# Batch 1's keys and values loaded behind the first units, their maxima taken by TensorE, and an undivided fp32 value product in a fused attention and feed-forward kernel

## The chip, the cores and the metric

The kernel runs on one core of a Trainium2 chip. The metric is device time in microseconds (us) of one execution; less is better. Three runs of the kernel before gave 734.79, 735.6 and 737.56 us, median 735.6 us.

## What is computed

Attention with a learned position bias, followed by a layer norm and a feed-forward block with a residual. There are 4 batches, 8 heads, 576 positions and a head size of 64; d_model is 512 and the feed-forward width 2048. Everything is float32. Cut to what matters:

```python
scores = scale * np.matmul(q, k.transpose(0, 1, 3, 2))
x = (psi_rel / psi_i)[..., None]            # logs of distances and positions
bias = np.maximum(x @ w1 + b1, 0.0) @ w2    # (576, 576, 8)
scores = scores + bias.transpose(2, 0, 1)[None]
attn = softmax(scores);  attn_out = np.matmul(attn, v)
x = attn_out.transpose(0, 2, 1, 3).reshape(B, S, H * D)
xn = (x - mu) / np.sqrt(var + 1e-06) * g_ln
out = x + np.maximum(xn @ w_ch1, 0.0) @ w_ch2
```

## The kernel before, in words

**Units.** Attention is done in 144 units. A unit is one batch, one chunk `c` of 128 query positions and one head; chunk 4 holds only 64 positions, so there a unit takes two heads. The list `ORD` sets their order: units 0 to 3 are batch 0's chunk 4, units 4 to 7 batch 1's chunk 4, units 8 to 15 batch 0's chunk 0, units 16 to 23 batch 1's chunk 0, and so on; batches 2 and 3 come from unit 72 on. One unit is: scores on PE (`qk`, L406, into `sps`), bias added and row minimum taken on DVE (L426, tile `t`), exponential on ACT (L430), transposition of the weights of attention, and the value product on PE into `xps` (`pv`).

**Bias.** The bias is worked out once, for all batches, in 36 groups of 16 rows: relu on ACT and DVE (`bias_relu`), fp32 matmuls on PE (`bias_mm`, L220 and L197, into `bps`), evacuation on ACT (`ev`), a DMA write to a DRAM buffer (`nb<-ev`). A unit reads its 128 x 576 piece back (`ldb<-nb`). Six groups are done ahead of the first unit, the others between the units.

**Value products of two kinds.** Where `nat_pv` holds (batch 0's chunks 4 and 0, batch 1's chunk 4, that is units 0 to 15) the values are used as they came, in fp32 (`vf`), with weights of attention transposed by PE; elsewhere the values are split into a high and a low fp16 part and PE does three times as many fp16 products (`pv_mms`, L497). In the fp32 kind `pv` takes the 128 query columns in two halves `e` of 64: five matmuls of 64 stationary columns for each half, so ten for a unit (L527).

**Splitting the values.** `split_v(b, g)` handles two heads' values. DVE reduces their absolute maximum along each partition (L365, `vam`); the maximum over partitions is taken for batches 0 and 1 by GpSimd (L369, a partition all-reduce into `var`), for batches 2 and 3 by PE and DVE in `part_max`: a PE transposition (L135), a DVE reduce (L138), a DVE product with a corner of the identity (`pdg`, L139), a PE matmul with a row of ones (L141), a DVE copy (L381). Its PSUM bank there is `y1` of `ps_y`, which the transposed weights of attention use too. Then follow some one-column operations on DVE (`pow2`, `c8`), the high part on ACT (L385) and the low part on DVE (L374). `w_scale` uses `part_max` too, once for each of four groups of feed-forward weights.

**Loads.** A sorted list `loads` says at which unit a tile is due, and `issue_loads(u)` issues what is due by `u + 6`. Keys (`kf`), values (`vf`, later `ldv`) and queries (`qf`) go through GpSimd's (POOL's) queue; bias pieces (`ldb`), bias writes (`nb`) and feed-forward weights (`wend`) through SP's. The keys of batches 0 and 1 are held back until a given one of the first six bias groups is evacuated (`gate`); the values are not. The pools of keys and values hold nine tiles each, so those of batches 0 and 1 fit at once.

**Feed-forward.** For each block of 128 positions, `ffn_w1` does 48 fp16 matmuls at a time into the only bank of `ps_h` (`hps`, L719), ACT (L724) and DVE (L727) read it out, and `ffn_w2` does 12 matmuls into `y` (L747). These are put between the units, so many a unit. The weights come packed and are unpacked (L653, L655, L657) and split (L692, L695) by DVE and ACT during the first 32 units.

The instructions of one engine run in the order in which they stand in its list. That order is not the order of the source: a scheduler lays the program out, so that a change in one place can move instructions in others.

Of the kernel before, what the change touches and what calls it, by code (L numbers as in the profile page):

```python
# [8 lines left out]
F32 = mybir.dt.float32  # L9
# [6 lines left out]
ALU = mybir.AluOpType  # L16
# [6 lines left out]
def kernel(  # L23
# [58 lines left out]
    id_sb = const.tile([128, 128], F32)  # L82
    one_sb = const.tile([2, 128], F32)
    gs_sb = const.tile([128, 512], F32)
# [49 lines left out]
    def part_max(am, n, ps):  # L134
        T.transpose(ps[0:n, 0:128], am, id_sb)  # L135
        mx = small.tile([2, 1], F32, tag="pmx", name="pmx")
        dg = small.tile([2, 2], F32, tag="pdg", name="pdg")
        V.tensor_reduce(out=mx[0:n], in_=ps[0:n, 0:128], op=ALU.max, axis=AX.X)  # L138
        V.tensor_scalar(out=dg[0:n, 0:n], in0=id_sb[0:n, 0:n], scalar1=mx[0:n], scalar2=None,  # L139
                        op0=ALU.mult)  # L140
        T.matmul(out=ps[:, 128:128 + n], lhsT=one_sb[0:n], rhs=dg[0:n, 0:n], start=True, stop=True)  # L141
        return ps[:, 128:128 + n]

    rt = {}
    evi, ttri = {}, {}
# [127 lines left out]
    for b in range(NB):  # L273
        if b < 2:
            tf = ustart[b, 4] == ub[b]
            for g in range(4):
                loads.append((ub[b] + (g if tf else 2 * g) - (3 if b == 0 else 4), "k", (b, g)))
                if npt[b]:
                    loads.append((ub[b] + ((-3, -1, 0, 1) if tf else (-3, 1, 3, 5))[g], "w", (b, g)))
        else:  # L280
            for g in range(4):
                loads.append((ub[b] + 2 * g - 8, "k", (b, g)))
        if not npt[b] or not KEEPV[b]:
            for g in range(4):
                loads.append((uv[b] - 13 + 3 * g, "v", (b, g)))
        for c in range(4):
            for hh in range(2):
                loads.append((ustart[b, c] + 4 * hh - 3, "q", (b, c, hh)))
        loads.append((ustart[b, 4] - 3, "q", (b, 4, 0)))
# [5 lines left out]
    def issue_loads(u):  # L295
# [4 lines left out]
        while loads and out_ld[0] < LD and loads[0][0] <= u + 6:  # L300
            need, kind, key = loads[0]
            if kind == "k":
# [3 lines left out]
                if gate_on[0]:  # L306
                    gate.append((ld, 1 * key[1] + 0 + 2 * key[0]))
                kt[key] = raw
                continue
            if kind == "q":  # L310
# [11 lines left out]
            if kind == "w":  # L322
# [4 lines left out]
                if gate_on[0]:  # L327
                    gate.append((ld, 0 * key[1] + -9 + 0 * key[0]))
                vraw[key] = raw
                continue  # L330
            if kind == "b":
# [25 lines left out]
    def split_v(b, g):  # L357
# [8 lines left out]
        if kept and 0:  # L366
            after(red, evi[gorder[min(NP, 0 + 6) - 1]])
        if kept:
            G.partition_all_reduce(ar, am, channels=128, reduce_op=bass_rust.ReduceOp.absmax)  # L369
# [9 lines left out]
        def hi():  # L379
            if not kept:  # L380
                V.tensor_copy(ar, part_max(am, 1, ps_y.tile([128, 512], F32, tag="y1", name="pmv")))  # L381
            pow2(ar, vs, None)
# [130 lines left out]
    def pv(u):  # L513
# [7 lines left out]
        if c < 4:  # L521
            if nat_pv(b, c):
                vf = vraw[b, h // 2].rearrange("p (a b c) -> p a b c", a=2, b=5)[:, h % 2]
                for e in range(2):
                    for j in range(5):
                        n = 128 if j < 4 else 64
                        T.matmul(out=o[64 * e:64 * e + 64, h, :],  # L527
                                 lhsT=p[0:n, 128 * j + 64 * e:128 * j + 64 * e + 64],
                                 rhs=vf[0:n, j], start=(j == 0), stop=(j == 4))
            else:  # L530
                pv_mms([(o[:, h, :], p, vt[b, h // 2][:, h % 2])])
# [291 lines left out]
    if True:  # L823
# [16 lines left out]
        V.memset(mhalf, -0.5)  # L840
        V.memset(one_sb, 1.0)
        V.memset(half2, 0.5)
# [173 lines left out]
```

## Time and profile before

| | us |
|---|---|
| runs (3) | 734.79, 735.6, 737.56; median 735.6 |
| profiled execution, its own time | 739.38 |
| its span in the profile | 737.6 |
| PE busy (matmuls) | 679.2 (92%) |
| DVE busy | 492.5 (67%) |
| ACT busy | 381.3 (52%) |
| POOL busy | 64.5 (9%) |

PE is TensorE's matmul side, PEld its weight loads, DVE VectorE, ACT ScalarE, POOL GpSimd, SP SyncE. A busy time is the time in which the engine had at least one instruction under way. The ends of matmuls are modelled, so the time from one start to the next tells more than the length of one. The span is the time from the first to the last instruction; the execution's own time is 1.8 us longer.

### The profile page before, as it was taken

The numbers are of one execution on the slowest core, as the hardware profiler recorded it, in microseconds if no ns is written. First come the engines' busy times: TensorE is split into PE (matmuls) and PEld (weight loads), VectorE is DVE, ScalarE is ACT, GpSimd is POOL, SyncE is SP. The second block draws the span as 40 slices with busy tenths as digits, with TensorE's granted clock in tenths as the row PEclk, the third lists the DMA queues.
The fourth block names the chain that finished last, engine by engine and source line by source line (L and its number), as shares of the span: only waits on it lengthen the run. The fifth ranks groups of instructions, "written<-read, shape, count | busy, mean of one in ns | idle before, by whom it ended". The sixth has DMA issues, their size and how long they took to land.

```text
span 737.6 us, 20228 instructions
## 1 busy us (share of the span) xinstructions
PE 679.2 (92%) x8308; PEld 471.7 (64%) x8308; DVE 492.5 (67%) x1168; ACT 381.3 (52%) x789; POOL 64.5 (9%) x120
## 2 busy tenths in 40 slices
PE   4299899798699999999999999999999999999994
PEld 3156666464455677777777777776777777776772
DVE  5657788887848576758777575777766765755221
ACT  4367796776659744445455444445444554441110
POOL 3400101100000000111100010100000000001000
PEclk9689999899999999999999999999999999999998
DMA  8987779799945697777876665857666866532100
GB/s 264 318 266 243 242 229 233 196 279 247 211 100 134 161 194 176 179 163 183 192 181 161 152 153 154 172 122 183 160 153 160 175 159 145 131 55 47 30 16 14
DMA packets 153680, 124.13 MB, mean 168 GB/s; under 512 B 118900, under 2 KB 119156, under 8 KB 153588
## 3 DMA queue, kind: packets, MB, share of 16 engines
q1 hardware_dynamic: 147154, 103.00, 57.7%
q0 software_dynamic: 5440, 19.40, 8.4%
q8 instruction: 65, 1.06, 0.6%
q10 hardware_dynamic: 994, 0.44, 0.2%
q14 instruction: 27, 0.22, 0.1%
HBM read 79.38 MB, written 15.63 MB: 129 GB/s over the span
## 4 chain that ended last, share of the span: by engine, by line
PE 78%; DMA 10%; DVE 5%; issue 3%; ACT 2%; POOL 1%; SPq 0%; ACTq 0%; POOLq 0%; DVEq 0%
PE hps L719 24%; PE y L747 23%; PE sps L406 10%; PE xps L497 7%; PE ptm L468 3%; PE bps L220 3%; DMA ldb<-nb 2%; DMA pt<-e 2%; PE bps L197 2%; DMA wend<-in_w_ch_dram 2%; DMA ldv<-in_v_p_dram 1%; PE xps L545 1%; DMA nb<-ev 1%; PE xps L527 1%; DMA b_sb<-in_b_r_dram 1%
## 5 line engine op out<-in xcount | busy, mean ns | idle before, releaser
L719 PE MATMUL hps<-xT,w 128*128 128x128 f16 x3240 | 201.0, 221 | 3.8 <-DVE w L695 2.4
L719 PEld LDWEIGHTS <-w 128*128 128x128 f16 x3240 | 186.7, 99 | 15.5 <-issue 7.0
L747 PE MATMUL y<-w,hh 128*128 128x512 f16 x810 | 188.1, 379 | 1.5 <-DVE x L758 1.1
L430 ACT ACTIVATE t<-t,m 128x576 f32<-128x576 f32 x144 | 111.0, 771 | 120.4 <-DVE m L426 120.3
L747 PEld LDWEIGHTS <-hh 128*128 128x128 f16 x864 | 79.6, 98 | 86.6 <-issue 2.2
L426 DVE CUSTOM_DVE_ANT_0 t<-sps,ldb 128x576 f32<-128x576 f32 x144 | 105.5, 752 | 14.7 <-PE sps L406 7.3
L406 PE MATMUL sps<-kf,qf 64*128 64x288 f32 (+1 forms) x640 | 100.8, 441 | 7.3 <-DMA kf<-in_k_s_dram 6.7
L497 PEld LDWEIGHTS <-pt 128*128 128x128 f16 (+1 forms) x1904 | 64.3, 100 | 40.9 <-issue 27.6
L724 ACT ACTIVATE hh<-hps 128x512 f16<-128x512 f32 x72 | 42.7, 593 | 84.1 <-PE hps L719 84.0
L497 PE MATMUL xps<-v,pt 128*128 128x64 f16 (+1 forms) x1904 | 77.0, 194 | 8.3 <-DMA pt<-e 8.3
L758 DVE SCALAR_TENSOR_TENSOR x<-y,ycs,x 128x512 f32<-128x512 f32 x72 | 53.8, 747 | 43.9 <-PE y L747 43.3
L727 DVE SCALAR_TENSOR_TENSOR hh<-hps,hh 128x512 f16<-128x512 f32 x72 | 49.4, 687 | 46.4 <-ACT hh L724 46.3
L406 PEld LDWEIGHTS sps<-kf,qf 64*128 64x128 f32 (+1 forms) x640 | 48.8, 178 | 35.8 <-issue 17.1
L473 ACT ACTIVATE pt<-ptm 128x512 f16<-128x512 f32 x56 | 33.2, 592 | 73.1 <-PE ptm L468 73.0
L482 DVE SCALAR_TENSOR_TENSOR e<-t,e 128x512 f16<-128x512 f32 x72 | 49.7, 690 | 22.2 <-ACT e L439 22.1
L179 ACT ACTIVATE r<-psi_sb,pr_sb 128x496 f32<-128x496 f32 (+31 forms) x91 | 53.0, 640 | 7.8 <-DVE pr_sb L123 4.0
L439 ACT ACTIVATE e<-t 128x576 f16<-128x576 f32 x72 | 48.7, 676 | 0.8
L316 POOL DMA_DIRECT2D qf<-in_q_main_dram x32 | 18.5, 579 | 335.7 <-PE sps L406 284.0
L476 DVE SCALAR_TENSOR_TENSOR pt<-ptm,pt 128x512 f16<-128x512 f32 x56 | 38.5, 687 | 8.6 <-ACT pt L473 8.5
L220 PE MATMUL bps<-r,nw_sb 128*32 128x296 f32 (+31 forms) x450 | 35.1, 374 | 4.1 <-DVE r L181 3.6
L468 PE MATMUL ptm<-id_sb,t 128*128 128x128 f32 x224 | 34.2, 275 | 0.8 <-ACT t L430 0.8
L468 PEld LDWEIGHTS ptm<-id_sb,t 128*128 128x128 f32 x224 | 25.9, 141 | 9.0 <-issue 2.1
(118 smaller groups left out, 664.8 us busy)
## 6 DMA issues: line engine op xcount, KB each, us to landing
ldb<-nb SPq DMA_DIRECT2D x128, 288.0 KB, 3.5
wend<-in_w_ch_dram SPq DMA_DIRECT2D x29, 512.0 KB, 4.9
nb<-ev SPq DMA_DIRECT2D x34, 296.0 KB, 3.9
qf<-in_q_main_dram POOLq DMA_DIRECT2D x32, 256.0 KB, 4.0
kf<-in_k_s_dram POOLq DMA_DIRECT2D x16, 288.0 KB, 5.5
ldb<-nb SPq DMA_DIRECT2D x32, 144.0 KB, 4.6
out_dram<-x SPq DMA_DIRECT2D x17, 256.0 KB, 2.1
vf<-in_v_p_dram POOLq DMA_DIRECT2D x8, 320.0 KB, 6.4
```

What stands on the lines that cost most here:

```text
L179: S.activation(r[:, 0:n], psi_sb[:, 0:n], AF.Relu, bias=pr_sb[:, g4:g4 + 1], scale=1.0)
L220: T.matmul(out=ps[32 * s:32 * s + 32, hf, a - lo:b - lo], lhsT=nw2_sb, rhs=src, start=True, stop=True)
L406: T.matmul(out=o, lhsT=l, rhs=kk, start=True, stop=True, tile_position=(64 * hf, 64 * e))
L426: ttri[u] = V.tensor_tensor_reduce(out=halves(t), in0=ps[:, :, 0:HS], in1=halves(bias), scale=-0.125, scalar=3e38, op0=ALU.add, op1=ALU.mi ...
L430: S.activation(t, t, AF.Exp, bias=m, scale=-1.0, accum_out=l8[b, c][:, h:h + 1])
L468: T.transpose(pm[:, 128 * j:128 * j + 128], t[:, 128 * j:128 * j + 128], id_sb)
L482: V.scalar_tensor_tensor(out=e16[:, 640:1152], in0=t[:, 0:512], scalar=E_SCALE, in1=e16[:, 0:512], op0=ALU.mult, op1=ALU.subtract)
L497: T.matmul(out=o, lhsT=p[:, m], rhs=v[:, j, a, :], start=(i == 0), stop=(i == len(ops) - 1))
L719: T.matmul(out=h[:, idx * n:idx * n + n], lhsT=w[:, wo + kk * 128:wo + kk * 128 + 128], rhs=xT[k][:, xo + kk, 0:n], start=(i == 0), stop=( ...
L727: V.scalar_tensor_tensor(out=hh[:, 1], in0=h, scalar=0.0, in1=hh[:, 0], op0=ALU.max, op1=ALU.subtract)
L747: T.matmul(out=yps[k][t], lhsT=hh[:, a, o:o + 128], rhs=w[:, wo:wo + 512], start=(f == f0 and i == 0), stop=(f == f1 - 1 and i == 2))
L758: V.scalar_tensor_tensor(out=x, in0=y, scalar=ycs[:, g:g + 1], in1=x, op0=ALU.mult, op1=ALU.add)
```

## The change

1. `loads`: keys of batch 1 are due at units 6, 6, 7, 7 in place of 0 to 3, its values at 7, 7, 8, 8 in place of 1, 3, 4, 5. They are issued while the first units run, and each waits for the newest L426 (`ttri`) of the program at that place.
2. `split_v`: GpSimd's all-reduce is kept for batch 0 only. Batch 1 goes through `part_max`, as batches 2 and 3 do, and all three use the bank of `ps_h` in place of `y1`.
3. `part_max`: the DVE product `pdg` and the row of ones are gone; PE takes the maximum itself, repeated 128 times, as stationary operand, and the corner of the identity as moving one.
4. `pv`, chunks 0 to 3: the fp32 value product is done with all 128 columns at once, five matmuls for a unit in place of ten. Of the units of this kind that holds for eight, 8 to 15. Chunk 4's are as they were.

```diff
     def part_max(am, n, ps):
         T.transpose(ps[0:n, 0:128], am, id_sb)
         mx = small.tile([2, 1], F32, tag="pmx", name="pmx")
-        dg = small.tile([2, 2], F32, tag="pdg", name="pdg")
         V.tensor_reduce(out=mx[0:n], in_=ps[0:n, 0:128], op=ALU.max, axis=AX.X)
-        V.tensor_scalar(out=dg[0:n, 0:n], in0=id_sb[0:n, 0:n], scalar1=mx[0:n], scalar2=None,
-                        op0=ALU.mult)
-        T.matmul(out=ps[:, 128:128 + n], lhsT=one_sb[0:n], rhs=dg[0:n, 0:n], start=True, stop=True)
+        T.matmul(out=ps[:, 128:128 + n], lhsT=mx[0:n].to_broadcast([n, 128]), rhs=id_sb[0:n, 0:n],
+                 start=True, stop=True)
         return ps[:, 128:128 + n]
...
             for g in range(4):
-                loads.append((ub[b] + (g if tf else 2 * g) - (3 if b == 0 else 4), "k", (b, g)))
+                loads.append((ub[b] + g - 3 if b == 0 else 6 + g // 2, "k", (b, g)))
                 if npt[b]:
-                    loads.append((ub[b] + ((-3, -1, 0, 1) if tf else (-3, 1, 3, 5))[g], "w", (b, g)))
+                    loads.append((ub[b] + (-3, -1, 0, 1)[g] if b == 0 else 7 + g // 2, "w", (b, g)))
...
+                if key[0] == 1:
+                    after(ld, ttri[max(ttri)])
...
-        if kept:
+        if b == 0:
             G.partition_all_reduce(ar, am, channels=128, reduce_op=bass_rust.ReduceOp.absmax)
...
-            if not kept:
-                V.tensor_copy(ar, part_max(am, 1, ps_y.tile([128, 512], F32, tag="y1", name="pmv")))
+            if b > 0:
+                V.tensor_copy(ar, part_max(am, 1, ps_h.tile([128, 512], F32, tag="h", name="pmv")))
...
-                for e in range(2):
-                    for j in range(5):
-                        n = 128 if j < 4 else 64
-                        T.matmul(out=o[64 * e:64 * e + 64, h, :],
-                                 lhsT=p[0:n, 128 * j + 64 * e:128 * j + 64 * e + 64],
-                                 rhs=vf[0:n, j], start=(j == 0), stop=(j == 4))
+                for j in range(5):
+                    n = 128 if j < 4 else 64
+                    T.matmul(out=o[:, h, :], lhsT=p[0:n, 128 * j:128 * j + 128],
+                             rhs=vf[0:n, j], start=(j == 0), stop=(j == 4))
```

What the scheduler makes of it shows in the engines' lists. A row there is a line of the kernel, an operation, its output and inputs, and the output's size; xN is N of them in a row. The line numbers of the changed kernel are some lower.

POOL's list, from the first load of a key on. Before: the keys of batch 0 and of batch 1 (and one tile of batch 2, in the ninth place of the pool), with the all-reduces among them.

```order
L305 DMA kf<-in_k_s_dram 128x576
L369 ISA
L369 ISA var<-vam 128x1 x2
L305 DMA kf<-in_k_s_dram 128x576
L369 ISA var<-vam 128x1
L305 DMA kf<-in_k_s_dram 128x576 x7
L369 ISA var<-vam 128x1 x5
```

The change, from the same place on: the four keys of batch 0 and two of batch 1, two values of batch 1, two more keys of batch 1 and that of batch 2, a query, the other two values.

```order
L302 DMA kf<-in_k_s_dram 128x576 x6
L324 DMA vf<-in_v_p_dram 128x640 x2
L302 DMA kf<-in_k_s_dram 128x576 x3
L315 DMA qf<-in_q_main_dram 128x512
L324 DMA vf<-in_v_p_dram 128x640 x2
```

No all-reduce stands between the keys any more, and batch 1's four values are no longer among the first loads but behind its keys.

DVE's list. Before, in the opening, ahead of the first unit: the maxima of the values among the relus of the bias.

```order
L365 TENSOR_REDUCE vam<-vf 128x1
L181 TENSOR_SCALAR rp<-psi_sb,npr_sb 128x560
L181 TENSOR_SCALAR r<-psi_sb,npr_sb 128x576 x2
L181 TENSOR_SCALAR r<-psi_sb,npr_sb 128x560 x2
L365 TENSOR_REDUCE vam<-vf 128x1
L112 TENSOR_SCALAR var<-var 128x1
L365 TENSOR_REDUCE vam<-vf 128x1
L112 TENSOR_SCALAR var<-var 128x1
L365 TENSOR_REDUCE vam<-vf 128x1
L181 TENSOR_SCALAR rp<-psi_sb,npr_sb 128x528
L112 TENSOR_SCALAR var<-var 128x1
L113 TENSOR_SCALAR vs<-var 128x1
```

The change, between unit 20's L426 and unit 21's (a piece of it): the maxima of the values stand among the unpacking and splitting of weights.

```order
L136 TENSOR_REDUCE pmx<-pmv 1x1
L366 TENSOR_REDUCE vam<-vf 128x1
L534 TENSOR_TENSOR x<-xps,rl 128x512
L654 SCALAR_TENSOR_TENSOR w_148<-wend,w_148 128x512
L694 SCALAR_TENSOR_TENSOR w_141<-w_142,ws,w_141 128x512
L483 SCALAR_TENSOR_TENSOR e_1647<-t,e_1647 128x512
L485 SCALAR_TENSOR_TENSOR e_1647<-t,e_1647 128x64
L178 TENSOR_SCALAR r<-psi_sb,npr_sb 128x304
L656 SCALAR_TENSOR_TENSOR w_147<-wend,w_147 128x512
L382 COPY var<-pmv 128x1
```

All eight reduces left the opening, batch 0's too, which the diff does not touch: four stand behind units 3 to 6 now, four behind units 15 to 20. Of the eight low parts of values (L374), one stood in the opening, five behind units 7 to 13 and two behind units 15 and 17; now all eight stand behind units 17 to 26.

PE's list, at the first of batch 2's maxima. Before: the transposition into `pmv` stands in the middle of 48 matmuls of `hps` (each with its weight load).

```order
L719 LDWEIGHTS w_145
L719 MATMUL hps<-xT,w_145 128x128
L135 MATMUL pmv<-id_sb,vam 1x128
L719 LDWEIGHTS w_145
L719 MATMUL hps<-xT,w_145 128x128
```

The change: it stands behind a block of `y`, with a unit's transposition and scores between.

```order
L746 MATMUL y_4905<-w_139,hh 128x512
L469 MATMUL ptm<-id_sb,t 128x128 x4
L407 MATMUL sps<-kf,qf 128x288 x4
L498 LDWEIGHTS pt
L498 MATMUL xps<-v,pt 128x64
L134 MATMUL pmv<-id_sb,vam 1x128
```

The matmul that ends this maximum in the change, 87 rows on, among the next unit's transpositions and scores:

```order
L498 LDWEIGHTS pt
L498 MATMUL xps<-v,pt 128x64
L469 MATMUL ptm<-id_sb,t 128x128
L137 MATMUL pmv<-id_sb,pmx 128x1
L469 MATMUL ptm<-id_sb,t 128x128 x3
L407 MATMUL sps<-kf,qf 128x288 x2
```

No `hps` stands between the two `pmv` instructions now; 27 value products, 12 matmuls of `y` and two score matmuls stand between them, and the next 48 of `hps` follow behind three transpositions, two score matmuls and 18 value products.

## Rows read from the trace of the kernel before

**Rows 1.** The page's busy times: engine, us (share of the span), instructions.

```profile
PE 679.2 (92%) x8308; PEld 471.7 (64%) x8308; DVE 492.5 (67%) x1168; ACT 381.3 (52%) x789; POOL 64.5 (9%) x120
```

**Rows 2.** Busy us by stretch: each engine (instructions), granted clock, DMA share, GB/s.

```profile
20.00:40.00 20.00, 6.34 (x72) 2.63 (x68) 12.94 (x43) 7.50 (x12) 7.69 (x16) 0.63 0.99 309
40.00:80.00 40.00, 36.83 (x394) 23.58 (x386) 25.10 (x60) 28.81 (x59) 1.92 (x3) 0.93 0.83 267
80.00:112.00 32.00, 30.50 (x347) 20.27 (x347) 28.43 (x65) 28.80 (x59) 4.10 (x5) 1.00 0.71 217
112.00:177.00 65.00, 56.69 (x667) 35.71 (x667) 54.39 (x132) 45.53 (x89) 6.98 (x9) 0.92 0.99 242
...
220.00:680.00 460.00, 459.16 (x5878) 331.03 (x5875) 317.00 (x746) 230.59 (x503) 35.11 (x69) 1.00 0.66 154
```

**Rows 3.** The chain that ended last, its first pieces: start us, us, what.

```profile
18.43 5.01 DMA nb<-ev
25.31 10.71 DMA ldb<-nb
37.48 4.22 PE bps L220 x48
```

**Rows 4.** DMA issues of 22 to 37 us, then of the page: count, KB, us to landing.

```profile
kf<-in_k_s_dram POOLq DMA_DIRECT2D x8, 288.0 KB, 8.3
...
ldb<-nb SPq DMA_DIRECT2D x32, 144.0 KB, 4.6
```

**Rows 5.** DVE in order of time: start us, us, instruction, [idle before it, what ended that].

```profile
14.02 1.52 DVE L365 TENSOR_REDUCE vam<-vf 128x1 f32<-128x640 f32 x2
36.15 0.76 DVE L426 CUSTOM_DVE_ANT_0 t<-sps,ldb 128x576 f32<-128x576 f32 x1 [2.15 <-DMA ldb<-nb]
38.62 0.76 DVE L426 CUSTOM_DVE_ANT_0 t<-sps,ldb 128x576 f32<-128x576 f32 x1 [1.30 <-DMA ldb<-nb]
```

**Rows 6.** PE in order of time: the scores of unit 4.

```profile
52.00 0.71 PE L406 MATMUL sps<-kf,qf 64*64 64x288 f32 x8
```

**Rows 7.** The chain: a fp32 value product, 48 matmuls, transpositions; weight loads by shape.

```profile
84.18 1.73 PE xps L527 x20
...
221.28 2.68 PE hps L719 x48
...
470.46 0.44 PE ptm L468 x4
...
478.26 0.44 PE ptm L468 x4
...
L527 PEld LDWEIGHTS xps<-vf,pt 128*64 128x64 f32 x128 | 8.7, 138 | 1.8 <-issue 1.0 <-PE ptm L452 0.2
L141 PEld LDWEIGHTS pmv<-pdg,one_sb 1*128 1x128 f32 x16 | 2.3, 182 | 0.9 <-DVE x L758 0.4
```

**Rows 8.** The chain of 470 to 560 us: the PE part of one maximum.

```profile
517.51 0.11 PE pmv L135
522.12 0.31 PE pmv L141 x2
```

**Rows 9.** DVE groups by shape: count, busy us, mean ns, idle before.

```profile
L365 DVE TENSOR_REDUCE vam<-vf 128x1 f32<-128x640 f32 x8 | 6.4, 806 | 0.0
L112 DVE TENSOR_SCALAR var<-var 128x1 f32<-128x1 f32 x16 | 2.3, 150 | 2.5 <-POOL var L369 2.2
L138 DVE TENSOR_REDUCE pmx<-pmv 1x1 f32<-1x128 f32 x8 | 2.2, 272 | 0.3 <-PE pmv L135 0.3
```

**Rows 10.** PE, then DVE, in order of time around one maximum of batch 3.

```profile
499.85 0.27 PE L135 MATMUL pmv<-id_sb,vam 128*1 128x128 f32 x1
504.42 0.38 PE L141 MATMUL pmv<-pdg,one_sb 1*128 1x1 f32 x2
...
502.09 0.67 DVE L727 SCALAR_TENSOR_TENSOR hh<-hps,hh 128x512 f16<-128x512 f32 x1
507.21 0.16 DVE L381 COPY var<-pmv 128x1 f32<-128x1 f32 x1
```

More of the change, by code (lines that the diff above doesn't have):

```diff
@@ L82 @@
     id_sb = const.tile([128, 128], F32)
-    one_sb = const.tile([2, 128], F32)
     gs_sb = const.tile([128, 512], F32)
@@ L329, in issue_loads @@
                 vraw[key] = raw
+                if key[0] == 1:
+                    after(ld, ttri[max(ttri)])
                 continue
@@ L840 @@
         V.memset(mhalf, -0.5)
-        V.memset(one_sb, 1.0)
         V.memset(half2, 0.5)
```

## The prediction

> **What bounds the kernel now.** I read the page's busy times first, then the busy time by stretch, then the chain of waits of the opening, and last the order of time and the groups by shape at the places that the change touches. PE has 679.2 us of work in a span of 737.6 [rows 1], so 58.4 us are idle on the engine that sets the end. The reader should see in the stretches [rows 2] where they lie. From 220 to 680 us PE is busy for 459.2 of 460 us: nothing there can be gained but PE work itself. Between 20 and 40 us it works 6.3 of 20 us, while the DMA engines are at 0.99. From 112 to 177 us (unit 17's L426 to unit 27's) it is idle for 8.3 us of 65; DVE has 54.4 us of work there and DMA is at 0.99, so PE is not alone. As the work of each unit is fixed, time won in the opening lasts only if DVE and PE can keep it up to 220 us; behind that, PE runs through.
>
> The opening's chain [rows 3]: the bias write lands at 23.4 us, the first unit's bias read is issued at 25.3 and needs 10.7 us, and DVE's first L426 starts at 36.15 after waiting for it [rows 5]; PE's next block follows at 37.5. The read is slow because of its company: in those 15 us eight keys of 288 KB (2.3 MB) are on the way too, 8.3 us each [rows 4]. On the page 144 KB reads take 4.6 us at the median.
>
> **The change, part by part.**
>
> *Loads, opening: -5.0 us.* Of the eight keys, five (batch 1's four and batch 2's one) are put behind the first units, and batch 0's others go out earlier, as no all-reduce and no batch 1 value is ahead of them in POOL's list. Then the read costs between its median of 4.6 us and what it costs now, 10.7 [rows 3, 4]: a gain between 6.1 and 0. I take 5.0, near the first end, as nearly half of the bytes go. The issue time of 25.3 stays, for the last early bias write stands ahead of the read in SP's list in both kernels. It is on the path: DVE waits for the read, PE for DVE.
>
> *Loads, later: +1.0 us.* Batch 1's keys and values (2.4 MB) now run between about 33 and 50 us. Behind them in POOL's queue stand queries that are due later. DMA is at 0.83 from 40 to 80 us [rows 2], and at the 309 GB/s of the stretch before 2.4 MB are 8 us of it. The first to want them is PE at unit 4's scores, at 52.0 us [rows 6], 13.4 us behind unit 1's L426 [rows 5], on which these loads wait; a load took 8.3 us in the crowd [rows 4]. So the keys come in time with 5 us to spare, and the cost is what weights and bias pieces lose in the crowd: 0 to 5 us (the whole gain of the opening). PE is the busy one there, 36.8 of 40 us, so I take 1.0.
>
> *Undivided value product: -4.2 us.* One product of a unit takes 1.73 us for 20 rows (ten fp32 matmuls, two rows each), 86 ns a row [rows 7]. It becomes ten rows with 128 stationary columns. How long is a row then? Not under the 86 ns of now. The fp32 transposition has 128 stationary columns and 128 moving ones, and goes at 110 ns a row (0.44 us for four); with 64 moving columns it would not be slower. The fp32 weight load shows 138 ns for 64 columns and 182 for 128 [rows 7]: 44 ns more, 130 ns a row. A unit then takes 0.86, 1.1 or 1.3 us, and eight units save 7.0, 5.0 or 3.4 us. I take 120 ns, 4.2 us; the lower end, 0, is the rival on the halves below. These units begin at 84 us; PE is at 30.5 of 32 us from 80 to 112 [rows 2].
>
> The Trainium skill (TensorE: Matmul & The Clock Gate, section LDWEIGHTS) gives a weight load as columns / 1.2 ns, so 53 ns more for 128 columns than for 64. By that a row would be 139 ns and the saving 2.7 us, and the sum 1.5 us higher; the difference of the two rows is 44 ns, so the trace bears its direction out, and its size nearly.
>
> *Maxima of batch 1 on PE: +1.7 us.* Four transpositions and four matmuls, 0.11 and 0.31 us [rows 8]. GpSimd's all-reduces were off the path.
>
> *DVE: +2.5 us.* The missing `pdg`, 12 operations of the size of a clamp (0.15 us [rows 9]), shortens a chain that nothing waits for. The rest is moved work. The opening loses the first two reduces at 14.0 us [rows 5] and six more, with clamps and scales; DVE was idle there for 7 us of 20 anyway [rows 2], so this saves nothing. Four of the eight reduces land behind units 3 to 6, where DVE has 25.1 us of 40 [rows 2] and room for them. Behind units 15 to 26 lands more: four reduces at 0.81 us, four reduces of maxima at 0.27 and their copies, some 18 one-column operations at 0.15, six low parts (counted like a reduce), together 3.2 + 1.7 + 2.7 + 4.8 = 12.4 us [rows 9]. In before's time that is 112 to 177 us, where DVE is idle for 10.6 us of 65 [rows 2]. If all idle time can be used, 1.8 us are left over; if none, 12.4. I take 2.5, near the first, since DVE's waits there are for weights that will have landed when it comes later.
>
> *The bank: +0.4 us.* `pmv` shares `hps`'s only bank now, 12 times. A maximum holds its bank from PE's transposition to DVE's copy: 499.85 to 507.37 us in one case [rows 10]. The change's list puts at least 1.5 us of other PE work between the last `pmv` matmul and the next `hps`. If the copy comes soon this costs nothing; it can cost far more (a rival).
>
> Sum: -5.0 + 1.0 - 4.2 + 1.7 + 2.5 + 0.4 = -3.6 us. The profiled execution took 739.4 us, 3.8 over the median of the runs; its 739.4 - 3.6 = 735.8 is 732.0 against the median of 735.6. **Forecast: 732.0 us**, 0.5% faster. 0.5%, 3.7 us, is about what a measurement of this kernel can tell from no change; the forecast stands on that line.
>
> **The rivals.**
>
> *All of it is kept, 725 us.* The opening gives its 6.1 us, the product 5.0, crowd, DVE and bank cost nothing: 735.6 - 6.1 - 5.0 + 1.7 = 726.2; with the product at 86 ns a row 724.2. For it: DVE's list up to unit 19 holds some 10 us less than before, and PE's half-rate clock (0.63 granted between 20 and 40 us [rows 2], a mean of 2.4 and 1.2 GHz, behind PE's idle time) would end sooner. Against: DVE is at 54.4 of 65 us just where the moved work lands.
>
> *DVE gives it back, 736 us.* If a third of its idle time between 112 and 177 us can be used, 12.4 - 3.5 = 9 us stay on the path; in place of 2.5 that is 6.4 more than the forecast, 738.4, and with the opening at 6.1 it is 737.3; if half can be used, 736.6 and 735.5. For it: DVE runs in order, and a wait of one instruction holds all behind it. Against: its waits are for loads that the delay lets land.
>
> *The halves already run side by side, 736 us.* The two halves write different partitions of one bank and use different columns of the array. Before, a row goes out every 86 ns, less than the 138 ns of its weight load [rows 7], so some loads do overlap. If that is due to the halves, a full-width row takes 173 ns, and the product saves nothing: 732.0 + 4.2 = 736.2. The transpositions speak against it: full width, a load of 141 ns or more, and a row every 110 ns. The Trainium skill (TensorEngine Tiling (Array Packing), Key Properties) says that tiles of the array can load and multiply in parallel; by that rule this rival holds.
>
> *The bank stops PE, 742 us.* One place: the eight maxima of batches 2 and 3, which fall between 220 and 680 us, where PE has no idle time [rows 2]. In 7.8 us (from one transposition to the next [rows 7]) PE fills the bank once with `hps`, for 2.7 us [rows 7], and DVE has read it 2.9 us later (499.85 to 502.76 [rows 10]); 2.2 us are free. A hold of 7.5 us is 5.3 too long. PE has other work meanwhile, but in a fixed order. If a quarter of the 5.3 is left uncovered, 1.3 us, eight times that is 10.6 us, less the 0.4 of the forecast: 742.2. It decides when the copy ends more than 1.5 us behind the last `pmv` matmul. In rows 10 it ended 2.6 us behind it (504.80 to 507.37), which speaks for this rival; against it, the scheduler put other work between `pmv` and `hps` in all cases.
>
> **How the numbers follow.** The forecast's case, with terms in their middles, 728 to 735 us: 0.42. All kept, under 728: 0.18. DVE gives it back, 735 to 739: 0.16. Halves side by side: 0.07. The bank stops PE, over 739: 0.17. Faster by over 0.5% means under 731.9: all of the second and six in ten of the first case, 0.43. Slower by over 0.5%, over 739.3: 0.17. The rest, 0.40, is within 0.5%. The range runs from 724, the best case with every term at its end, to 740, which leaves out most of the bank's 0.17.
>
> **What would show it.** The first L426 at about 31 us in place of 36.15, and a bias read of 5 us or so in the chain of the opening. L527 with 80 rows, 128 stationary columns, a unit in 1.1 to 1.3 us. DVE at over 90% between units 17 and 26, and PE idle there not more than 3 us longer than before. No wait of PE's `hps` for a copy of L381's kind over 0.5 us. From 220 us on PE busy throughout. I would be wrong if PE waits for a key of batch 1 at unit 4, if unit 27's L426 comes later than at 177 us, or if PE shows idle time between 220 and 680 us.

## The result and the profile after

The change made the kernel slower. Its four runs gave 743.57 to 755.24 us, median 749.84, against 736.58 for the kernel before (four runs). Ratios here and below leave out runs in a slower state, here that of 755.24, and this one is 1.0136, 95% interval [1.0093, 1.0179]. Six more runs of it beside new ones of the kernel before gave 1.0179 [1.0142, 1.0217]. 732.0 was forecast and 740 was the upper end of the range. The profiled execution is the fastest of its kind, 743.57 us, and so shows less than the medians do.

The busy times of the changed kernel, against [rows 1]:

```profile
PE 677.3 (91%) x8240; PEld 471.7 (64%) x8240; DVE 491.4 (66%) x1163; ACT 381.1 (51%) x789; POOL 62.4 (8%) x116
```

PE has 1.9 us less work here (the sum said 2.5), and the span is 4.2 us longer (741.8): PE is idle for 64.5 us in place of 58.4. The busy time by stretch shows where (columns as in [rows 2]):

```profile
20.00:40.00 20.00, 9.78 (x108) 4.58 (x98) 8.43 (x21) 10.15 (x17) 1.06 (x2) 0.66 0.98 315
40.00:80.00 40.00, 37.09 (x410) 25.12 (x410) 29.97 (x71) 25.57 (x56) 6.96 (x13) 1.00 0.90 299
112.00:177.00 65.00, 51.44 (x585) 33.94 (x581) 54.45 (x147) 42.49 (x80) 5.94 (x10) 0.89 0.83 203
...
220.00:680.00 460.00, 453.86 (x5822) 327.02 (x5821) 311.52 (x731) 229.60 (x502) 35.51 (x67) 1.00 0.65 154
```

From 20 to 40 us PE works 3.4 us more than before, which is the opening's gain. From 112 to 177 it is idle for 13.6 us in place of 8.3. From 220 to 680, where it had been idle for 0.8, it is idle for 6.1.

How far the units are tells when the time goes: starts of the bias add (L426, now L427), in us, from DVE in order of time. "Again" is the second profile of the changed kernel (span 749.8); c1 and d4 are experiments below. The profiled executions of c1 and d4 (739.01 and 740.95 us) are the fastest of their runs, whose medians are 743.64 and 747.24, so their columns show less than the medians too.

| unit | before | after | again | c1 | d4 |
|---|---|---|---|---|---|
| 0 | 36.15 | 32.16 | 31.05 | 32.16 | 36.40 |
| 3 | 47.22 | 46.58 | 49.32 | 49.75 | 46.67 |
| 19 | 129.84 | 120.67 | 123.04 | 122.65 | 129.05 |
| 21 | 140.16 | 141.89 | 145.15 | 144.88 | 140.18 |
| 32 | 213.36 | 212.71 | 219.16 | 213.89 | 208.84 |
| 36 | 237.81 | 238.10 | 244.55 | 239.28 | 233.26 |
| 140 | 651.38 | 655.45 | 663.53 | 650.60 | 652.69 |

Three steps of it. **Units 0 to 3:** 4 to 5 us ahead, and then nothing of it is left. DVE in order of time:

```profile
32.16 0.76 DVE L427 CUSTOM_DVE_ANT_0 t<-sps,ldb 128x576 f32<-128x576 f32 x1 [0.27 <-DMA ldb<-nb]
...
33.25 0.75 DVE L427 CUSTOM_DVE_ANT_0 t<-sps,ldb 128x576 f32<-128x576 f32 x1
...
39.13 0.43 DVE L652 TENSOR_SCALAR w<-wend 128x512 uint32<-128x512 uint32 x1 [5.12 <-DMA wend<-in_w_ch_dram]
...
41.33 0.75 DVE L427 CUSTOM_DVE_ANT_0 t<-sps,ldb 128x576 f32<-128x576 f32 x1
```

Bias and keys are no longer late; the third tile of packed weights is. DVE stands for 5.12 us, with unit 2 queued behind it.

**Units 19 to 21:** from 9.2 us ahead to 1.7 behind. These two units take 21.2 us (10.3 before); from 128 to 142 us, between units 20 and 21, DVE is busy for 13.7 of 14.0 us: 7.2 with unpacking and low parts of weights, 2.0 with the maxima of values that moved here. This group of weights' low parts starts at 127 us in both kernels, so part of the lead at unit 19 is work that had not come yet. Behind unit 21 DVE waits for GpSimd, and PE's bias product waits for DVE: DVE, POOL and PE in order of time:

```profile
147.91 0.15 DVE L111 TENSOR_SCALAR var<-var 128x1 f32<-128x1 f32 x1 [4.21 <-POOL var L370]
...
147.47 1.09 POOL L370 PARTITION_ALL_REDUCE var<-vam  x3 [6.81 <-issue]
...
150.80 1.11 PE L194 MATMUL bps<-r,nw_sb 128*32 128x305 f32 x8 [4.57 <-DVE r L178]
```

Among PE's waits from 112 to 220 us these three are new (what waited, for what: us in total, times, longest):

```profile
PE bps L194 <- DVE r L178: 7.1, 2, 4.6
PE hps L718 <- DVE var L382: 2.1, 1, 2.1
PE pmv L137 <- DVE pmx L136: 1.0, 2, 0.6
```

The last two belong to batch 1's maxima in the bank of `hps`: the next `hps` waits for the copy, and PE for the reduce of a maximum. In c0 they are 2.1 and 2.3 us, in c1 2.1 and 3.8.

**Units 36 to 140:** 413.6 us before, 417.4 after, 419.0 in the second profile. The waits of PE in 220 to 680 us (before there was one, 0.8 us):

```profile
PE y L746 <- ACT hh L723: 1.6, 3, 0.9
PE pmv L134 <- DVE hh L726: 1.5, 3, 0.9
PE sps L407 <- DVE m L427: 1.2, 2, 0.6
PE pmv L137 <- DVE pmx L136: 0.9, 1, 0.9
PE xps L498 <- DVE x L534: 0.4, 1, 0.4
PE hps L718 <- DVE var L382: 0.3, 1, 0.3
```

The chain that ended last runs through one of them. It reaches back to 533.7 us only, and from this point on PE runs through to 679 us:

```profile
541.59 0.69 DVE e L483
542.28 0.14 DVE e L485
542.42 0.61 DVE hh L726
543.03 0.04 issue
543.07 0.27 PE pmv L134
```

DVE's read of `hps` frees the bank, and PE's transposition into `pmv` has stood waiting for it, ahead of value products that need nothing of it.

### The profile page after: what moved, and what is told of

It reads as the page before. It is cut to its first block, busy times and chain, and to the rows that moved or that the text cites. A ratio compares the mean times of both kernels' runs of the same rounds, so it can differ in the third digit from the quotient of the medians.

```text
span 741.8 us, 20075 instructions
## 1 busy us (share of the span) xinstructions
PE 677.3 (91%) x8240; PEld 471.7 (64%) x8240; DVE 491.4 (66%) x1163; ACT 381.1 (51%) x789; POOL 62.4 (8%) x116
## 3 DMA queue, kind: packets, MB, share of 16 engines
q8 instruction: 64, 1.05, 0.6%
## 5 line engine op out<-in xcount | busy, mean ns | idle before, releaser
L718 PE MATMUL hps<-xT,w 128*128 128x128 f16 x3240 | 196.0, 220 | 3.8 <-DVE var L382 2.4
L746 PE MATMUL y<-w,hh 128*128 128x512 f16 x810 | 191.1, 381 | 2.5 <-ACT hh L723 1.6
L718 PEld LDWEIGHTS <-w 128*128 128x128 f16 x3240 | 184.2, 98 | 12.7 <-issue 7.9
L427 DVE CUSTOM_DVE_ANT_0 t<-sps,ldb 128x576 f32<-128x576 f32 x144 | 105.5, 749 | 8.0 <-DMA ldb<-nb 3.7
L407 PE MATMUL sps<-kf,qf 64*128 64x288 f32 (+1 forms) x640 | 97.0, 435 | 7.2 <-ACT ev L220 3.5
L498 PEld LDWEIGHTS <-pt 128*128 128x128 f16 (+1 forms) x1904 | 67.0, 101 | 43.4 <-issue 27.9
L407 PEld LDWEIGHTS sps<-kf,qf 64*128 64x128 f32 (+1 forms) x640 | 47.4, 175 | 32.5 <-issue 10.2
L217 PE MATMUL bps<-r,nw_sb 128*32 128x296 f32 (+31 forms) x450 | 37.1, 373 | 3.6 <-DVE r L178 1.5
L470 DVE SCALAR_TENSOR_TENSOR e16t<-t,e16t 128x64 f16<-128x64 f32 x56 | 12.0, 214 | 27.6 <-ACT e16t L437 27.6
```

The lines of the kernel that those rows point to most:

```text
L407: T.matmul(out=o, lhsT=l, rhs=kk, start=True, stop=True, tile_position=(64 * hf, 64 * e))
L427: ttri[u] = V.tensor_tensor_reduce(out=halves(t), in0=ps[:, :, 0:HS], in1=halves(bias), scale=-0.125, scalar=3e38, op0=ALU.add, op1=ALU.mi ...
L498: T.matmul(out=o, lhsT=p[:, m], rhs=v[:, j, a, :], start=(i == 0), stop=(i == len(ops) - 1))
L718: T.matmul(out=h[:, idx * n:idx * n + n], lhsT=w[:, wo + kk * 128:wo + kk * 128 + 128], rhs=xT[k][:, xo + kk, 0:n], start=(i == 0), stop=( ...
L746: T.matmul(out=yps[k][t], lhsT=hh[:, a, o:o + 128], rhs=w[:, wo:wo + 512], start=(f == f0 and i == 0), stop=(f == f1 - 1 and i == 2))
```

## The experiments

Theory B: the bank shared with `hps`. Theory D: DVE's work moved behind units 16 to 26. Theories P (GpSimd) and L (late loads) came with the runs. Ratios are to runs of the kernel before on the same chip; 0.1% is 0.74 us.

### The bank

c0 is the changed kernel again, unedited; c1 is the change with one edit (the diffs of this part are cut to what matters).

> The changed kernel once more, for a second profile and a narrower interval: its four runs lay between 743.6 and 755.2 us. Theory D (DVE): the kernel is some 9 us ahead of the one before at unit 19, and the work of DVE that moved behind units 16 to 26 takes that away by unit 32. Theory B (bank): the bank that the maxima now share with hps stops PE, above all from 220 us on, where PE was idle 0.8 us before and 6.1 us in the first profile. Both expect 745 to 752 us here, and a second profile with the same signs: ahead by 6 us or more at unit 18 or 19, level within 3 us at unit 32, PE idle for 4 us or more between 220 and 680 us.

```diff
-  part_max(am, 1, ps_h.tile([128, 512], F32, tag="h", name="pmv"))
+  part_max(am, 1, ps_h.tile([128, 512], F32, tag="h", name="pmv") if b == 1
+           else ps_y.tile([128, 512], F32, tag="y1", name="pmv"))
```

> The change, with the maxima of batches 2 and 3 back in the bank y1 and only batch 1's in that of hps. Theory B: PE idle between 220 and 680 us falls from 6.1 to under 1.5 us, and the time falls by 5 us against the changed kernel. Theory D: what was lost is lost by unit 32, and the time stays within 2 us of the changed kernel's; units 18 to 32 as in the changed kernel.

d4, the kernel before with one edit:

```diff
-  part_max(am, 1, ps_y.tile([128, 512], F32, tag="y1", name="pmv"))
+  part_max(am, 1, ps_h.tile([128, 512], F32, tag="h", name="pmv"))
```

> The kernel before, with one edit: the maxima of batches 2 and 3 in the bank of hps. Theory B: 4 to 6 us over the kernel before, PE idle for 4 us or more between 220 and 680 us. Theory D: nothing, within 1.5 us.

Measured: c0 1.0179, c1 1.0071 [1.0041, 1.0101], d4 1.0105 [1.0064, 1.0145]. PE's stretch of 220 to 680 us in c0, c1 and d4:

```profile
220.00:680.00 460.00, 452.42 (x5740) 325.05 (x5740) 311.09 (x734) 233.31 (x510) 35.51 (x67) 1.00 0.66 155
```

```profile
220.00:680.00 460.00, 460.00 (x5885) 331.50 (x5884) 315.81 (x737) 230.27 (x504) 34.86 (x69) 1.00 0.66 154
```

```profile
220.00:680.00 460.00, 453.86 (x5805) 327.79 (x5804) 312.77 (x735) 225.78 (x495) 35.36 (x66) 1.00 0.67 153
```

PE is idle for 7.6, 0.0 and 6.1 us there. The bank for batches 2 and 3 alone costs 5 to 8 us: 5.3 by d4's idle time (6.1 less the 0.8 of before), 5.9 by units 36 to 140 of d4 (419.4 against 413.6), 7.8 by the ratios (d4, and c0 less c1 comes to 8). Theory B holds; c1's remaining 0.7%, 5.2 us, is something else. c0 was 6.8 us ahead at unit 19 as expected, but 5.8 behind at unit 32, not level within 3.

### The other parts one by one

c3 gives batch 1's maxima back to GpSimd in the changed kernel; d3 is the kernel before with the late loads alone (the two hunks on `loads` and `after(ld, ...)`); e1 is c1 with the loads of before; d1 is the kernel before with the product's hunk, e2 with that and `part_max`'s hunk.

```diff
-        if b == 0:
+        if kept:
             G.partition_all_reduce(ar, am, channels=128, reduce_op=bass_rust.ReduceOp.absmax)
...
-            if b > 0:
+            if not kept:
```

> The change, with the maxima of batch 1 on GpSimd again, so without PE, DVE and the bank for these four. By DVE's list the low parts of the values then stand behind units 6 to 18 again, not 17 to 26. Theory D: the lead of the opening is kept, unit 32's bias add comes 5 us or more ahead of the kernel before (213.4 us), and the time is 8 to 12 us under the changed kernel's. Theory B: only the four maxima of batch 1 leave the bank, so at most 3 us under the changed kernel.

> The kernel before, with the late loads of batch 1's keys and values as its one edit; all maxima of batches 0 and 1 stay on GpSimd. Theory L: slower by 8 us or more; GpSimd's eight all-reduces now stand between the first units and hold its list, as in the run with all else of the change and these maxima on GpSimd, where PE waited 8.0 us for GpSimd's winv at 90 us and unit 32 came 15 us late. Theory D: the opening's 4 us are kept, as the low parts stay behind units 6 to 18; 2 to 5 us faster than before.

> All of the change except the late loads and the bank for batches 2 and 3: batch 1's keys and values are loaded as before, its maxima go through PE and the bank of hps. By DVE's list the low parts of the values stand behind units 17 to 26 here too. Theory D (the work that moved behind units 17 to 26 costs time by itself): slower than before by 5 us or more, and unit 27's bias add at 182 us or later (177.3 before). Theory L (the late loads cost it, since the opening's gain is lost at once to the next late transfer and what was done while DVE waited there has to be done later): no slower than before, within 2 us.

> The kernel before, with the undivided fp32 value product of units 8 to 15 as its one edit. In the profile of the change a unit's ten rows take 1.4 to 1.5 us from the first start to the last end, where twenty took 1.8 to 2.0. If PE sets the time in those units, 3 us faster than before; if its waits for DVE and DMA by unit 32 take it up, 0 within 1 us.

> The kernel before, with the undivided value product and the maximum without the product on DVE and the row of ones; loads, GpSimd's all-reduces and the bank as before. Expected: as the undivided product alone within 1 us, as the maxima of batches 2 and 3 hold up nothing in the bank y1; so 0 to 3 us faster than before. It is also the version most likely to beat both kernels.

| run | ratio | interval |
|---|---|---|
| c3 | 1.0261 | [1.0219, 1.0303] |
| d3 | 1.0208 | [1.0172, 1.0243] |
| e1 | 1.0106 | [1.0073, 1.0139] |
| d1 | 0.9982 | [0.9952, 1.0012] |
| e2 | 0.9994 | [0.9967, 1.0022] |

The undivided product alone gains 1.3 us, not clear of none, and the simpler maximum nothing that these intervals show. Theory D's account of c3 and d3 was wrong by its sign: with the low parts back in their old places they are the slowest. d3 came out as theory L had said, 15 us over. e1 is over by what theory D had said (5 us or more, unit 27 at 197.5), but with a wait that neither theory had named, so it doesn't decide between them. It also has 6.0 us of the lead at unit 19 (123.81) with the loads of before: most of that lead is not the loads'. In d3 PE waits for GpSimd's `winv` (POOL, then PE in order of time); in e1 likewise, for 13.65 us at 160.4:

```profile
91.70 0.73 POOL L677 TENSOR_TENSOR winv<-winv,half 128x2 f32<-128x2 f32 x1 [8.57 <-issue]
...
92.49 0.37 PE L135 MATMUL gram<-id_sb,winv 128*2 128x128 f32 x1 [7.94 <-POOL winv L677]
```

```profile
159.60 0.73 POOL L668 TENSOR_TENSOR winv<-winv,half 128x2 f32<-128x2 f32 x1 [7.28 <-issue]
...
160.38 0.37 PE L134 MATMUL gram<-id_sb,winv 128*2 128x128 f32 x1 [13.65 <-POOL winv L668]
```

"Issue" is time in which the engine waited for nothing that the profile shows. It appears where GpSimd comes from an all-reduce or goes to one. That made theory P.

### GpSimd's pause

g1 is the kernel before with one all-reduce more:

```diff
+        def extra():
+            xr = const.tile([128, 1], F32, name="xr")
+            xi = G.partition_all_reduce(xr, w1_sb, channels=128, reduce_op=bass_rust.ReduceOp.absmax)
+            after(xi, ttri[16])
+
+        at(18, extra)
```

> The kernel before, with one more all-reduce on GpSimd, of a small constant into a tile that nobody reads, behind unit 16's bias add (108 us) and ahead of the second winv (111 us) in GpSimd's list. Theory P: when GpSimd goes from its other work to an all-reduce or back it stands still for 6 to 9 us; one all-reduce here brings two such pauses, so the second winv comes at 122 us or later in place of 111.1, PE waits for it for 6 us or more, and the time grows by 5 to 10 us. Rival: an all-reduce costs what its row shows, 0.4 us; winv comes at 112 us and the time stays within 1.5 us.

Measured 1.0100 [1.0066, 1.0134]. POOL, then PE in order of time:

```profile
114.29 0.46 POOL L881 PARTITION_ALL_REDUCE xr<-w_sb  x1 [10.97 <-DVE m L426]
123.02 0.73 POOL L673 TENSOR_TENSOR winv<-winv,half 128x2 f32<-128x2 f32 x1 [8.27 <-issue]
...
123.81 0.37 PE L135 MATMUL gram<-id_sb,winv 128*2 128x128 f32 x1 [8.31 <-POOL winv L673]
```

An all-reduce of 0.46 us costs PE 8.31 us and the kernel 7.4. Theory P holds, as a mechanism. All kept traces bear it out: the 18 profiles with all-reduces have 40 changes between all-reduces and other work, and in none does GpSimd's next operation start less than 5.6 us behind the end of the one before. Each change begins with two instructions of another name, here those of g1 (times, ns each, first and last start):

```profile
L881 POOLq MODIFY_POOL_CONFIG  x2: 38/38/38, 103.6 to 103.6; - x2
...
L673 POOLq MODIFY_POOL_CONFIG  x2: 83/83/83, 114.7 to 114.7; - x2
```
f2 and f4 are c1 and e1 with batch 0's reduces and all-reduces (here `maxima`) written ahead of the first unit; f1 is c1 with batch 0's maxima on PE too, so without any all-reduce (the diff is cut to the call).

```diff
+        for g in range(4):
+            amr[g] = maxima(0, g, vraw[0, g])
         qk(0)
```

> The change with the late maxima in y1 (the run that was 0.7% over the kernel before), and batch 0's reduces and all-reduces put ahead of the first unit, as they stood before. Low parts stay behind units 17 to 26. Theory P: GpSimd has no pause behind the opening, DVE no wait for its maxima; 3 to 6 us less than that run, so level with the kernel before within 0.4%. Theory D (the moved work of DVE by itself): no gain, 0.5% or more over the kernel before.

> The same with the loads as before: undivided product, simplified maximum, batch 1's maxima through PE, batch 0's all-reduces ahead of the first unit. Without the last it was 1.06% over the kernel before, with PE waiting 13.7 us for a winv that stood behind the all-reduces. Theory P: that wait goes; 5 to 8 us less, within 0.4% of the kernel before. Theory D: low parts are where they were, so 0.6% or more over the kernel before.

> The change with the late maxima in y1, and no all-reduce at all: batch 0's maxima go through PE and the bank of hps too. By DVE's list five low parts move on, to behind units 26 to 31. Theory P: no pause of GpSimd at all; 2 to 5 us under the run with the late maxima in y1, level with the kernel before within 0.5%. Theory D: more work behind units 20 to 31, so slower than that run, 1% or more over the kernel before.

Measured: f2 1.0060 [1.0034, 1.0086], f4 1.0084 [1.0047, 1.0121], f1 1.0047 [1.0019, 1.0075]. Theory P expected f2 and f4 within 0.4% of the kernel before, and that fails: 0.1 and 0.2 points off c1 and e1, inside the intervals. f1 is within the 0.5% that it expected, 1.8 us under c1 where 2 to 5 were, and not at the 1% or more of theory D, which had f2 and f4 right. In f4 the 13.65 us are gone, and PE waits 5.8 us for an earlier `winv`. In f2 DVE no longer waits for an all-reduce (3.1 us in c1) and PE waits 0.4 us for `winv`, so GpSimd's pause isn't shown to be what is left in c1. f2 and f4 differ by the loads alone: the late loads gain 0.2 points, within -0.2 and 0.7.

### The place of the low parts

The fp16 tile of a pair of heads needs the one spare buffer of the value pool's nine, so by the program the low parts follow one another, and a late first maximum delays all eight. h1 and h2 are f2 and f4, h3 is f1, with batch 1 split eight steps earlier:

```diff
-                    at(u0 - 4 + 2 * g, lambda b=b, g=g: split_v(b, g))
+                    at(u0 - 4 + 2 * g if b == 0 else 4 + 2 * g, lambda b=b, g=g: split_v(b, g))
```

> The kernel with late maxima in y1 and batch 0's all-reduces ahead of the first unit (0.6% over the kernel before), with batch 1's split started at steps 4 to 10 in place of 12 to 18. By DVE's list the low parts then stand behind units 8 to 18, as before. Theory D: the 0.6% goes, and with the late loads and the undivided product the time is within 0.3% of the kernel before or under it. Rival (PE's maxima and hps waiting for their bank cost it wherever they stand): still 0.5% or more over.

> The same with the loads as before (0.84% over the kernel before with the late split). Theory D: within 0.3% of the kernel before. Rival: still 0.6% or more over it.

> The kernel without all-reduces, late maxima in y1 (0.47% over the kernel before), with batch 1's split started at steps 4 to 10. Its four low parts move to behind units 9 to 15; batch 0's stay behind units 26 to 31. Theory D: about half is regained, 0.1 to 0.4% over the kernel before. Rival: no gain, 0.5% or more.

Measured: h1 1.0015 [0.9981, 1.0049], h2 1.0207 [1.0157, 1.0257], h3 1.0195 [1.0143, 1.0247]. h1 came out level, as theory D said; its interval overlaps f2's. In it PE waits 0.3 us for the bias relu of L178 from 112 to 220 us, against 6.6 in c1. h2 and h3 miss by far. h2 has the pause again (9.45 us ahead of the first `winv`, PE waits 7.7 us). h3 has no all-reduce and no such wait; its granted clock is 0.76 from 112 to 177 us (0.92 in [rows 2]), and its cause stays open. Theory D is borne out by one run of three.

### The opening's gain

h4 is h1, h5 is d1, with the packed weights unpacked later:

```diff
-                if wdec and 32 - len(wdec) < 1 + (100 * u) // 100:
+                if wdec and 32 - len(wdec) < max(0, u - 1) + (u > 4) + (u > 8):
```

> The kernel that came out level with the one before (late loads, undivided product, batch 0's all-reduces early, batch 1's split at steps 4 to 10, late maxima in y1), with the packed weights unpacked two units later in the opening and one unit later up to unit 8. If the third weight tile is what ate the opening's gain, unit 3's bias add comes at 45 us or earlier (47.2 before, 48.9 in that kernel), and the time is 0.3 to 0.8% under the kernel before; if the DMA engines are simply full there, the wait moves to another load, unit 3 stays at 47 us or later and the time within 0.3%.

> The kernel before with the undivided product (0.18% under the kernel before, not clear of noise) and the same later unpacking. Expected: unit 0 still at 36 us or later, as the keys of both batches crowd the opening; time within 0.4% of the kernel before, and over h4's by 2 us or more if the late loads are worth something once the weights give way.

Measured: h4 1.0148 [1.0107, 1.0189], h5 0.9963 [0.9933, 0.9993]. h4 was 2.5 us ahead of the kernel before at unit 4 and 4.0 at unit 11, then 8.5 behind at unit 12: GpSimd's way back from the all-reduces stood behind two queries, and PE waited 7.3 us for `winv`. Unit 3 came at 46.69, between the two limits that were set (45 and 47), and behind a wait for a weight tile again; DVE, then PE in order of time:

```profile
45.36 0.43 DVE L656 TENSOR_SCALAR w<-wend 128x512 uint32<-128x512 uint32 x1 [6.45 <-DMA wend<-in_w_ch_dram]
...
85.69 0.37 PE L134 MATMUL gram<-id_sb,winv 128*2 128x128 f32 x1 [7.25 <-POOL winv L676]
```

So later unpacking moved the wait for weights and did not end it. h5 is within its 0.4%, and 1.9 points under h4 where 2 us over it would have spoken for the late loads. h6 adds one operation to h4, to bring GpSimd back early (cut to the operation):

```diff
+        def back():
+            after(G.tensor_tensor(out=scr, in0=half2[:, 0:1], in1=half2[:, 0:1], op=ALU.pow), ttri[0])
+
+        at(0, back)
```

> The last kernel with late loads and later unpacking, and one added operation: a power of one column on GpSimd behind unit 0's bias add, into a tile that nobody reads, so that GpSimd is back from the all-reduces before the queries and winv. Theory P: no pause ahead of the first winv, no wait of PE for it over 2 us, unit 12's bias add before 87 us (85.3 before, 93.8 without this), and 6 to 10 us less than that run (749.6): 0.4% over to 0.5% under the kernel before. If the pause is not what spoiled it: unit 12 at 90 us or later and 1% or more over the kernel before.

Measured 1.0052 [1.0030, 1.0075], 741.97 us against h4's 749.55. The first `winv` in h4, and in h6 with the added operation (POOL in order of time):

```profile
84.90 0.73 POOL L676 TENSOR_TENSOR winv<-winv,half 128x2 f32<-128x2 f32 x1 [9.08 <-issue]
```

```profile
30.88 0.78 POOL L892 TENSOR_TENSOR scr<-half 128x1 f32<-128x1 f32 x1 [11.07 <-DVE m L431]
...
77.30 0.72 POOL L676 TENSOR_TENSOR winv<-winv,half 128x2 f32<-128x2 f32 x1 [0.84 <-DVE winv L674]
```

A useless operation of 0.78 us takes 7.6 us off (7.0 by the ratios, as the two ran on different chips), within the 6 to 10 expected; the time is 0.1 points above its range. Unit 12 comes at 85.95. By unit 14 it is 8.8 us behind the kernel before, with a granted clock of 0.72 from 80 to 112 us; that wasn't pursued. Of all versions only h5 has an interval under the kernel before, at 0.37%: below what one measurement of this kernel can tell, and the interval only just leaves out no change.

## Why the prediction was wrong

**Loads, opening (-5.0): right at unit 0.** The first bias add is 4.0 to 5.1 us earlier, and bias reads land in 5.0 us at the median between 22 and 37 us.

**Loads, later (+1.0): the first step that failed.** The text said "the cost is what weights and bias pieces lose in the crowd: 0 to 5 us (the whole gain of the opening)" and took 1.0, because PE was busy from 40 to 80 us. It was the 5: at unit 3 the lead is 0.6 us in one profile, and the second is 2.1 late. Versions with the loads of before have unit 3 at 46.67 (d4) to 49.78 us (d1), so the lead is gone within their spread. Unit 4's keys, which I had looked at, were in time. DMA is at 0.98 from 20 to 40 us (0.99 before): with the engines full, to move one load back was to let the next one decide. By f2 and f4 the two terms together, -4.0 in the sum, come to some -1.8 (not clear of none).

**Undivided product (-4.2): right as PE work, not as time.** A unit's ten rows, PE in order of time, and the loads by shape:

```profile
92.84 1.00 PE L527 MATMUL xps<-vf,pt 128*128 128x64 f32 x8
93.68 0.27 PE L454 MATMUL ptl<-id_sb,t 128*64 128x128 f32 x1
93.88 0.43 PE L527 MATMUL xps<-vf,pt 64*128 64x64 f32 x2
94.24 0.41 PE L665 MATMUL gram<-w 128*128 128x128 bf16 x4
...
L527 PEld LDWEIGHTS xps<-vf,pt 128*128 128x128 f32 x64 | 8.1, 198 | 0.5 <-issue 0.4
```

From start to start the eight rows take 0.84 us and the two behind the transposition 0.36: 1.20 for ten, 120 ns a row, as taken, and 0.53 less than the 1.73 of before. Over the eight units the rows take 10.2 us in place of 14.1 (from each start to the next instruction, idle time left out), 3.9 less. Within the eight rows a row starts 112 ns behind the last, the pace of the transposition and not the 130 ns that the two weight loads gave. The Trainium skill (TensorE: Matmul & The Clock Gate, section LDWEIGHTS) gives a weight load as columns / 1.2 ns; the prediction's estimate from it, 139 ns a row, was too high. The load alone, 107 ns for 128 columns by that rule (an estimate), is near the 112 ns between rows, though a load shows 198 ns here. The rival of halves side by side falls: a full row would have taken 173 ns. Of the 3.9 us d1 kept 1.3 (-0.9 to 3.6).

**Batch 1's maxima on PE (+1.7): right.** Their instructions take 2.0 us of PE, by the same measure. PE's busy time in all can't be read so finely: 677.3 and 682.8 us in two profiles of the changed kernel.

**DVE (+2.5): the second step that failed.** "DVE's waits there are for weights that will have landed when it comes later": its busy time from 112 to 177 us stayed at 54.45 of 65 (54.39 before), not over 90%, and PE still lost 5.3 us more there than before. What I had added up was work; what cost was the order. DVE ran full just where units 20 and 21 needed it and stood idle behind it, and PE's bias product waited 7.1 us for DVE's relu, a wait that it had not had. Unit 27 came at 185.7, where 177 had been the limit. e1 puts a price on batch 1's maxima on PE without the late loads: 1.06 points, with GpSimd's pause in it; h1 is level in another order, 0.6 points under c1 (0.1 to 1.0), while h2 and h3 are not. Without the bank the sum was -4.0, and c1 measured +5.2: 9 us, of which the product and the loads, by d1 and by f2 and f4, come to some 5. Which share is whose isn't settled.

**GpSimd: left out.** "GpSimd's all-reduces were off the path" was not quite true of the kernel before. Its own trace had the pause, in the opening, and DVE waited 2.19 us for its end; on the way back PE waited 2.62 us for the first `winv` (POOL, DVE, PE in order of time):

```profile
21.73 0.76 POOL L369 PARTITION_ALL_REDUCE var<-vam  x2 [7.24 <-issue]
...
22.17 0.15 DVE L112 TENSOR_SCALAR var<-var 128x1 f32<-128x1 f32 x1 [2.19 <-POOL var L369]
...
75.65 0.27 PE L135 MATMUL gram<-id_sb,winv 128*2 128x128 f32 x1 [2.62 <-POOL winv L673]
```

In the change batch 0's all-reduces stand between two `winv` (104.92 and 164.48 us); no term priced that. It is in the 4.57 us that PE waited behind unit 21, but without it (f2) the time was only 0.1 points under c1's, inside the intervals. In five other versions (c3, d3, e1, h2, h4) PE waits 7 to 14 us for a `winv` behind it. The Trainium skill (GPSIMD Engine Reference, section Instruction dispatch) says that the first call of freshly loaded GpSimd code pays some 6 us that show as no instruction. The pauses that show as "issue" here took 5.6 to 9.8 us, both to the all-reduce and back, so the trace agrees in kind and is mostly longer.

**The bank (+0.4): the third step that failed, and the largest.** It cost 5 to 8 us for batches 2 and 3. The rival that "the bank stops PE" had the place and the sign, a price (10.6) above what was measured, and mostly the wrong side of the bank: from 220 us on the next `hps` waited for the copy for 0.3 us only (1.1 in c0, 0.7 in d4). For batch 1, which the rival left out, its side was right: 2.1 us, where the sign set in the prediction was 0.5. From 220 us on the transposition into `pmv` waits for DVE's read of the `hps` ahead of it, and what is queued behind it starts late, with the waits for `hh` and the minimum that follow. The list showed `pmv` behind `y`; I asked how long `pmv` holds the bank, and not who holds it when `pmv` comes.

Two rivals came in together, "DVE gives it back" and "the bank stops PE", each weighed alone in the prediction. The profiled execution was 4.2 us longer than that of before: 0.3 by unit 36 and 3.8 from there to unit 140. By the medians the parts add up: c1's 0.71 and d4's 1.05 points make 1.76, and c0 measured 1.79.

**What the medians have on top** is the spread of the changed kernel. Its two profiles, of one program, have spans of 741.8 and 749.8 us; the second has a granted clock of 0.91 from 40 to 80 us and 0.88 from 177 to 220, the first 1.00 in both. Mean clocks of 0.974 and 0.965, as a mix of 2.4 and 1.2 GHz, are 39 and 52 us at the lower level; 14 us more at half speed are worth at most 7 us of PE work (an estimate from these two means), nearly the 8.0 between them. That is not all: another run of the changed kernel took 748.42 us at the same 0.974. From 40 to 112 us PE was idle for 7.4 us in the second, for 5.9 in the first. Whether the idle time brought the lower clock or both come from late loads wasn't tried.

## What to carry to other kernels

Where an engine has no idle time, ask of every shared buffer that a step is moved to both questions: how long the step holds it, and who holds it when the step comes; the instruction that waits delays all that is queued behind it. A gain at the head of a stage whose DMA engines are full was worth little here, and the next late transfer has to be named and priced first. And in GpSimd's list count the changes between all-reduces and other work: each stood it still for 5.6 us or more here, and one small operation at a place where nothing waits took a 9 us pause off the path.

## What was unexpected of the hardware

GpSimd's pause, 5.6 to 9.8 us behind two MODIFY_POOL_CONFIG with no other instruction shown, against the 0.46 us that g1's all-reduce itself takes. It can hide behind a wait: in g1 the way to the all-reduce fell within a wait of 10.97 us for DVE, and only the way back, 8.27 us, was seen as "issue".
